# One 16 KB-per-partition K load per batch, with the key permutation moved into exp's write

## The chip, the cores and the metric

The kernel runs on one core of one Trainium2 chip. The metric is device microseconds; lower is better. The span of a profile, from the first to the last instruction, is a little shorter or longer than a run's time. A run over 1.5% above the fastest run of its kernel counts as slow, and ratios leave it out. A difference of less than 2% counts as "same", also where its interval excludes 1. "The Trainium skill" is a set of notes on the chip that readers may have; its pages are named by their titles.

## The reference

A decode step of grouped-query attention over a filled cache. There are 32 batches, 4 query tokens each, 32 query heads on 4 K/V heads, 2048 keys, head dimension 128, everything in bf16.

```python
q = (x @ wq).reshape(B, Sq, Hq, Dh).transpose(0, 2, 1, 3)
k = jnp.repeat(k_cache, rep, axis=1)
v = jnp.repeat(v_cache, rep, axis=1)
scores = jnp.einsum("bhqd,bhkd->bhqk", q, k) * (Dh ** -0.5)
p = softmax(scores, axis=-1)
o = jnp.einsum("bhqk,bhkd->bhqd", p, v)
return o.transpose(0, 2, 1, 3).reshape(B, Sq, Hq * Dh) @ wo
```

## The kernel before

For each batch i, PE computes QK for the batch into four PSUM banks. VectorE (DVE) takes the row maximum, and ScalarE (ACT) computes exp into P in SBUF. PE multiplies P's blocks by a diagonal matrix, which transposes and normalizes them. PV and a small eviction follow. In between, PE transposes the K of batch i+2 in eight "fills" of eight 128x128 blocks. These go through a ring of four PSUM banks, from which DVE and ACT evict them. K is double buffered, V is three deep, and wo is loaded in pieces along the way.

```python
def k_src(b):
    return k_cache[b].rearrange("g (p t) d -> p g (t d)", p=128)
def v_src(b):
    return v_cache[b].rearrange("g (p t) d -> p g (t d)", p=128)
# ... sync engine: K of batch b, one load of 4 KB per partition for each head
for g in range(G):
    eng.dma_start(K_sb[:, ks, g, :], k_src(b)[:, g, :]).then_inc(s_k[ks][g], 16)
# ... PE, in each batch
for c in range(Sk // 512):
    for g in range(G):
        eng.matmul(ps_s[32*g:32*(g+1), c*512:(c+1)*512],
                   lhsT=QT_sb[:, i, REP*g:REP*(g+1), :],
                   rhs=KT_sb[:, kts, g, c*512:(c+1)*512],
                   start=True, stop=True, tile_position=(0, 32*g))
if i >= 1:
    do_pv(i - 1)
if i + KT_AHEAD < B:
    do_kt_fills(i + KT_AHEAD)     # waits for a head's load at every second fill
do_tr_fills(i)                    # waits for exp
# ... ACT
ins = eng.activation(P_sb, ps_s[:, :], ACT.Exp,
                     bias=negmx[:, i:i+1], scale=scale, accum_out=ssum[:, i:i+1])
# ... cut: Q projection, evictions, output projection
```

Of the kernel before, what the change touches and what calls it, by code (L numbers as in the profile page):

```python
# [8 lines left out]
BF16 = mybir.dt.bfloat16  # L9
# [15 lines left out]
def bass_standalone__gqa_block_cached__sampling_kernel(  # L25
# [9 lines left out]
    _, Hkv, Sk, Dh = k_cache.shape  # L35
# [6 lines left out]
    NKT = Sk // 128  # L42
    G = Hkv
    scale = float(Dh) ** -0.5
    NKB = 2
    NVB = 3
    NKTB = 2
# [127 lines left out]
    with ExitStack() as es:  # L175
        w_sb = es.enter_context(nc.sbuf_tensor("w_sb", [128, KT, Hq * Dh], BF16))
        wq_sb = w_sb
        wo_view = w_sb[:, :, :].rearrange("p a (c n) -> p (a c) n", n=D)
        K_sb = es.enter_context(nc.sbuf_tensor("K_sb", [128, NKB, G, NKT * Dh], BF16))
        V_sb = es.enter_context(nc.sbuf_tensor("V_sb", [128, NVB, G, NKT * Dh], BF16))  # L180
        KT_sb = es.enter_context(nc.sbuf_tensor("KT_sb", [128, NKTB, G, Sk], BF16))
        QT_sb = es.enter_context(nc.sbuf_tensor("QT_sb", [128, B, Hq, Sq], BF16))
        oT_sb = es.enter_context(nc.sbuf_tensor("oT_sb", [128, Hq, NT], BF16))
        pp_sb = es.enter_context(nc.sbuf_tensor("pp_sb", [128, 2, Sk], BF16))
        P_sb = pp_sb[:, 0, :]
# [11 lines left out]
        ps_s = es.enter_context(nc.psum_tensor("ps_s", [128, Sk], F32))  # L197
# [9 lines left out]
        s_wq = [es.enter_context(nc.semaphore(f"s_wq{i}")) for i in range(NWQC)]  # L207
        s_wo = es.enter_context(nc.semaphore("s_wo"))
        s_out = es.enter_context(nc.semaphore("s_out"))
        s_k = [[es.enter_context(nc.semaphore(f"s_k{i}_{g}")) for g in range(G)] for i in range(NKB)]  # L210
        s_v = [es.enter_context(nc.semaphore(f"s_v{i}")) for i in range(NVB)]
        s_pe = es.enter_context(nc.semaphore("s_pe"))
        s_dve = es.enter_context(nc.semaphore("s_dve"))
# [5 lines left out]
        def wait_ev(eng, name):  # L219
            e, n = ev[name]  # L220
            eng.wait_ge(sems[e], n)

        def mark_ev(e, ins, name):
            n = counters[e].mark(ins)
            assert ev[name] == (e, n), (name, ev[name], e, n)
# [1 line left out]
        block = es.enter_context(nc.Block())  # L227

        def k_src(b):
            return k_cache[b].rearrange("g (p t) d -> p g (t d)", p=128)  # L230

        def v_src(b):
            return v_cache[b].rearrange("g (p t) d -> p g (t d)", p=128)
# [39 lines left out]
        @block.sync  # L273
        def _(eng):
            eng.dma_start(x_sb, x_flat[:, :]).then_inc(s_x, 16)
            wq_v = wq.rearrange("(kt p) n -> p kt n", p=128)
            for c in range(NWQC):
                eng.dma_start(wq_sb[:, :, c * WQC:(c + 1) * WQC], wq_v[:, :, c * WQC:(c + 1) * WQC]).then_inc(s_wq[c], 16)  # L278
            for b in range(KT_AHEAD, B):
                ks = b % NKB  # L280
                wait_ev(eng, ("fill", job_index[("kt", b - NKB, KT_FILLS - 1)]))
                for g in range(G):
                    eng.dma_start(K_sb[:, ks, g, :], k_src(b)[:, g, :]).then_inc(s_k[ks][g], 16)  # L283
            wait_ev(eng, "out_evac0")
            wait_ev(eng, "out_evac1")
            eng.dma_start(out_flat[:, :], out_sb).then_inc(s_out, 16)
            eng.wait_ge(s_out, 16)

        @block.tensor
        def _(eng):  # L290
# [8 lines left out]
            def do_kt_fills(b):  # L299
                ks = b % NKB  # L300
                for f in range(KT_FILLS):
                    j = job_index[("kt", b, f)]
                    if f % 2 == 0:
                        eng.wait_ge(s_k[ks][f // 2], 16 * (b // NKB + 1))
                    ring_wait(j)
                    if j == 2:
                        wait_ev(eng, "xT_evac")
                    g, half = f // 2, f % 2
                    dst = ring_bf16[j % NRING]
                    for q in range(8):  # L310
                        t = half * 8 + q
                        ins = eng.transpose(  # L312
                            dst[:, q * 128:(q + 1) * 128],
                            K_sb[:, ks, g, t * Dh:(t + 1) * Dh],
                            ident[:, :],
                        )
                    mark_ev("pe", ins, ("fill", j))
# [68 lines left out]
            for i in range(B):  # L386
                kts = i % NKTB
                for f in range(KT_FILLS):
                    wait_ev(eng, ("evac", job_index[("kt", i, f)]))
                if i == 0:  # L390
                    wait_ev(eng, f"q_evac{Hq // 4 - 2}")
                    wait_ev(eng, f"q_evac{Hq // 4 - 1}")
                else:
                    wait_ev(eng, f"exp{i - 1}")
                for c in range(Sk // 512):
                    for g in range(G):
                        ins = eng.matmul(  # L397
                            ps_s[32 * g:32 * (g + 1), c * 512:(c + 1) * 512],
                            lhsT=QT_sb[:, i, REP * g:REP * (g + 1), :],
                            rhs=KT_sb[:, kts, g, c * 512:(c + 1) * 512],  # L400
                            start=True,
                            stop=True,
                            tile_position=(0, 32 * g),
                        )
                mark_ev("pe", ins, f"qk{i}")
# [3 lines that stand above are left out]
                    do_kt_fills(i + KT_AHEAD)  # L409
                do_tr_fills(i)  # L410
# [5 lines left out]
            for c in range(2):  # L416
                for h in range(Hq):
# [3 lines left out]
                        rhs=wo_view[:, h, c * 512:(c + 1) * 512],  # L421
# [5 lines left out]
        def emit_evac(eng, e, j):  # L427
            kind, b, f, cons = jobs[j]
            assert cons == e
            wait_ev(eng, ("fill", j))  # L430
            if kind == "kt":
                kts = b % NKTB
                g, half = f // 2, f % 2
                if b >= NKTB:
                    wait_ev(eng, f"qk{b - NKTB}")
                src = ring_bf16[j % NRING]
                dst = KT_sb[:, kts, g, half * 1024:(half + 1) * 1024]
            else:
                if b > 0:
                    wait_ev(eng, f"pv{b - 1}")  # L440
                src = ring_f32[j % NRING]
                dst = PT_sb[:, 4 * f:4 * f + 4, :].rearrange("p a b -> p (a b)")
            if e == "dve":
                ins = eng.tensor_copy(dst, src)  # L444
            else:
                ins = eng.activation(dst, src, ACT.Copy)  # L446
            mark_ev(e, ins, ("evac", j))
# [64 lines left out]
        @block.scalar  # L512
        def _(eng):
            for b in range(KT_AHEAD):
                for g in range(G):
                    eng.dma_start(K_sb[:, b % NKB, g, :], k_src(b)[:, g, :]).then_inc(s_k[b % NKB][g], 16)
            def act_q_evac(j):
                bank = j % 4
                wait_ev(eng, f"qproj_bank{j}")
                src = ps_s[:, bank * 512:(bank + 1) * 512].rearrange("p (hh b s) -> p hh b s", hh=4, b=B, s=Sq)  # L520
                dst = QT_sb[:, :, 4 * j:4 * j + 4, :].rearrange("p b hh s -> p hh b s")
                ins = eng.activation(dst, src, ACT.Copy)  # L522
                mark_ev("act", ins, f"q_evac{j}")

            for f in range(KT_FILLS):
                if kt_consumer(f) == "act":
                    emit_evac(eng, "act", job_index[("kt", 0, f)])
            for j in range(1, Hq // 8, 2):
                act_q_evac(j)
            for f in range(KT_FILLS):  # L530
                if kt_consumer(f) == "act":
                    emit_evac(eng, "act", job_index[("kt", 1, f)])
            for j in range(Hq // 8 + 1, Hq // 4, 2):
                act_q_evac(j)
            for i in range(B):
                wait_ev(eng, f"negmax{i}")
                if i > 0:
                    wait_ev(eng, ("fill", job_index[("tr", i - 1, TR_FILLS - 1)]))
                ins = eng.activation(  # L539
                    P_sb,  # L540
                    ps_s[:, :],
                    ACT.Exp,
                    bias=negmx[:, i:i + 1],
                    scale=scale,
                    accum_out=ssum[:, i:i + 1],
                )
                mark_ev("act", ins, f"exp{i}")
                if i + KT_AHEAD < B:
                    for f in range(KT_FILLS):
                        if kt_consumer(f) == "act":  # L550
                            emit_evac(eng, "act", job_index[("kt", i + KT_AHEAD, f)])
                for f in range(TR_FILLS):
                    if tr_consumer(f) == "act":
                        emit_evac(eng, "act", job_index[("tr", i, f)])
            wait_ev(eng, "oproj1")
            ins = eng.activation(out_sb[:, 512:1024], ps_s[:, 512:1024], ACT.Copy)
            mark_ev("act", ins, "out_evac1")
# [30 lines left out]
```

## Time and profile before

| | before |
|---|---|
| median time | 409.33 us |
| DMA rate, 100 to 350 us | 407 GB/s |
| exp, one batch | 1967 ns |
| QK, mean of one matmul | 391 ns |
| start to first QK | 47.7 us |
| first to last QK, 31 batches | 330.6 us (10.7 us each) |
| last QK to the end | 31.3 us |

The first fence has lines of the profile's page. Rows of 40 signs are 40 equal slices of the span. PEclk is PE's granted clock and DMA the busy share of the 16 engines, both in tenths; GB/s is what they moved. The `q1` line gives the packets of the hardware queue, the MB, and the share of the engines' time. The line with `DMA 53%` is the chain of work that ended last, by engine. Group lines give busy us and mean ns of one, then the idle time of the engine before it and who ended it.

```profile
PEclk9799799998999899999999999997998989889679
DMA  8999999999999999999999999999999999997000
GB/s 307 400 387 401 408 408 407 407 406 407 407 407 408 405 406 407 406 407 407 408 404 407 407 407 406 407 407 406 407 406 407 407 407 408 403 402 308 38 2 26
...
q1 hardware_dynamic: 21728, 71.84, 44.7%
...
DMA 53%; PE 28%; issue 6%; SPq 5%; DVE 4%; ACT 3%; ACTq 0%; DVEq 0%
...
L539 ACT ACTIVATE pp_sb<-ps_s,negmx 128x2048 bf16<-128x2048 f32 x32 | 62.9, 1967 | 98.7 <-DVE negmx L484 98.7
L481 DVE TENSOR_REDUCE mx<-ps_s 128x1 f32<-128x2048 f32 x32 | 73.3, 2292 | 43.8 <-PE ps_s L397 43.8
...
L397 PE MATMUL ps_s<-KT_sb,QT_sb 128*32 128x512 bf16 x512 | 34.7, 391 | 2.6 <-ACT QT_sb L522 0.8
```

DMA is the limit: 9 tenths and about 407 GB/s in almost every slice. The groups show engines that are each busy for a small part of a batch. The 16 QK matmuls of a batch overlap: each lasts 391 ns on average, and all of them together 1.05 us.

The second fence is the timeline of one batch: start in us, length in us, engine and line, what it does. In brackets is the idle time before it and what ended it.

```profile
205.20 1.05 PE L397 MATMUL ps_s<-KT_sb,QT_sb 128*32 128x512 bf16 x16
...
206.30 2.29 DVE L481 TENSOR_REDUCE mx<-ps_s 128x1 f32<-128x2048 f32 x1 [1.32 <-PE ps_s L397]
...
208.81 1.97 ACT L539 ACTIVATE pp_sb<-ps_s,negmx 128x2048 bf16<-128x2048 f32 x1 [3.01 <-DVE negmx L484]
...
211.32 0.25 DVE L498 TENSOR_SCALAR diag<-ident,rinv 128x128 bf16<-128x128 bf16 x1
...
212.85 0.62 PE L312 MATMUL ps_c<-ident,K_sb 128*128 128x128 bf16 x8 [1.32 <-DMA K_sb<-in_k_cache_dram]
...
215.93 1.05 PE L397 MATMUL ps_s<-KT_sb,QT_sb 128*32 128x512 bf16 x16
```

The two QK lines (205.20 and 215.93) are 10.7 us apart. Maximum, exp and diagonal follow each other without slack, and at 212.85 PE waits 1.3 us for the K of a coming batch. Where data was prefetched, at 47.7, 56.7 and 65.7 us, QKs came 9.0 us apart. So this loop has, by estimate, some 1.7 us of slack per batch (10.7 less 9.0).

### The profile page before, as it was taken

To read this page: it belongs to the slowest core of one execution; us is meant where nothing else is said; L and a number is where in the kernel's file an instruction comes from. 1 tells how busy PE (TensorE), PEld (TensorE's weight loads), DVE (VectorE), ACT (ScalarE), POOL (GpSimd) and SP (SyncE) were. 2 spreads that over 40 slices of the span, in tenths; PEclk is the share of its full clock that TensorE was granted. 3 is DMA by queue.
4 is the path that set the end of the run, shared out by engine and by line. 5 is a ranking of instruction groups with operands and counts; after the bars stand their busy time and mean duration, and the time that the engine had idled before them with its cause. 6 is when DMAs were issued, how large, how long until landed. Compare 5 with 4: busy or idle time off the path is not lost.

```text
span 409.6 us, 12650 instructions
## 1 busy us (share of the span) xinstructions
PE 306.7 (75%) x5448; PEld 251.4 (61%) x5448; DVE 244.7 (60%) x390; ACT 197.2 (48%) x230; POOL 42.0 (10%) x70
## 2 busy tenths in 40 slices
PE   4576877988777687577777777759876787775596
PEld 4476766867655576466666566548765676674442
DVE  2113286786666587677766776745875867765400
ACT  1213066474555555555555455553555555545300
POOL 0001011110100111111111111110110111120000
PEclk9799799998999899999999999997998989889679
DMA  8999999999999999999999999999999999997000
GB/s 307 400 387 401 408 408 407 407 406 407 407 407 408 405 406 407 406 407 407 408 404 407 407 407 406 407 407 406 407 406 407 407 407 408 403 402 308 38 2 26
DMA packets 42390, 152.33 MB, mean 372 GB/s; under 512 B 3168, under 2 KB 3168, under 8 KB 42336
## 3 DMA queue, kind: packets, MB, share of 16 engines
q0 software_dynamic: 19456, 75.50, 46.3%
q1 hardware_dynamic: 21728, 71.84, 44.7%
q10 hardware_dynamic: 1152, 4.19, 2.6%
q8 instruction: 44, 0.72, 0.7%
q14 instruction: 10, 0.08, 0.1%
HBM read 151.26 MB, written 0.26 MB: 370 GB/s over the span
## 4 chain that ended last, share of the span: by engine, by line
DMA 53%; PE 28%; issue 6%; SPq 5%; DVE 4%; ACT 3%; ACTq 0%; DVEq 0%
DMA K_sb<-in_k_cache_dram 32%; DMA V_sb<-in_v_cache_dram 15%; DMA w_sb<-in_wq_dram 6%; PE ps_o L346 5%; PE ps_s L418 4%; PE ps_o L312 4%; PE ps_s L397 3%; SPq L278 3%; PE ps_c L312 3%; PE ps_a L312 3%; PE ps_b L312 2%; SPq L283 2%; ACT KT_sb L446 2%; DVE mx L481 2%; PE ps_s L371 2%
## 5 line engine op out<-in xcount | busy, mean ns | idle before, releaser
L539 ACT ACTIVATE pp_sb<-ps_s,negmx 128x2048 bf16<-128x2048 f32 x32 | 62.9, 1967 | 98.7 <-DVE negmx L484 98.7
L481 DVE TENSOR_REDUCE mx<-ps_s 128x1 f32<-128x2048 f32 x32 | 73.3, 2292 | 43.8 <-PE ps_s L397 43.8
L346 PEld LDWEIGHTS ps_o<-pp_sb,V_sb 128*128 128x128 bf16 x2048 | 53.9, 96 | 25.9 <-issue 16.6
L346 PE MATMUL ps_o<-pp_sb,V_sb 128*128 128x32 bf16 x2048 | 57.4, 178 | 11.5 <-DMA V_sb<-in_v_cache_dram 7.0
L312 PE MATMUL ps_c<-ident,K_sb 128*128 128x128 bf16 x512 | 43.6, 232 | 19.7 <-DMA K_sb<-in_k_cache_dram 15.1
L268 POOL DMA_DIRECT2D V_sb<-in_v_cache_dram x32 | 23.8, 745 | 303.1 <-PE ps_o L346 274.4
L312 PE MATMUL ps_a<-ident,K_sb 128*128 128x128 bf16 x512 | 43.3, 232 | 13.7 <-issue 7.6
L444 DVE COPY KT_sb<-ps_b 128x1024 bf16<-128x1024 bf16 x64 | 43.7, 684 | 12.0 <-PE ps_b L312 11.9
L446 ACT ACTIVATE KT_sb<-ps_a 128x1024 bf16<-128x1024 bf16 x32 | 32.6, 1019 | 37.1 <-PE ps_a L312 37.0
L312 PE MATMUL ps_b<-ident,K_sb 128*128 128x128 bf16 x512 | 43.9, 233 | 7.9 <-issue 7.9
L312 PEld LDWEIGHTS ps_c<-ident,K_sb 128*128 128x128 bf16 x512 | 34.1, 105 | 21.6 <-DMA K_sb<-in_k_cache_dram 19.5
L312 PE MATMUL ps_o<-ident,K_sb 128*128 128x128 bf16 x512 | 43.1, 232 | 3.2 <-DVE KT_sb L444 3.1
L312 PEld LDWEIGHTS ps_a<-ident,K_sb 128*128 128x128 bf16 x512 | 32.9, 104 | 17.6 <-issue 12.0
L446 ACT ACTIVATE KT_sb<-ps_c 128x1024 bf16<-128x1024 bf16 x32 | 32.7, 1022 | 20.9 <-PE ps_c L312 20.9
L312 PEld LDWEIGHTS ps_b<-ident,K_sb 128*128 128x128 bf16 x512 | 34.7, 105 | 9.1 <-issue 8.5
L312 PEld LDWEIGHTS ps_o<-ident,K_sb 128*128 128x128 bf16 x512 | 34.2, 105 | 6.9 <-DVE KT_sb L444 4.4
L444 DVE CAST pp_sb<-ps_a 128x512 bf16<-128x512 f32 x32 | 22.1, 691 | 27.2 <-PE ps_a L328 27.2
L397 PE MATMUL ps_s<-KT_sb,QT_sb 128*32 128x512 bf16 x512 | 34.7, 391 | 2.6 <-ACT QT_sb L522 0.8
L446 ACT ACTIVATE KT_sb<-ps_o 128x1024 bf16<-128x1024 bf16 x32 | 32.7, 1023 | 0.0
L444 DVE COPY KT_sb<-ps_a 128x1024 bf16<-128x1024 bf16 x32 | 21.9, 685 | 10.2 <-PE ps_a L312 10.2
L371 PE MATMUL ps_s<-pp_sb,w_sb 128*128 128x128 bf16 x256 | 19.8, 255 | 10.0 <-DMA w_sb<-in_wq_dram 10.0
L371 PEld LDWEIGHTS ps_s<-pp_sb,w_sb 128*128 128x128 bf16 x256 | 19.2, 118 | 10.6 <-DMA w_sb<-in_wq_dram 10.6
(36 smaller groups left out, 288.9 us busy)
## 6 DMA issues: line engine op xcount, KB each, us to landing
V_sb<-in_v_cache_dram POOLq DMA_DIRECT2D x32, 2048.0 KB, 26.4
K_sb<-in_k_cache_dram SPq DMA_DIRECT2D x120, 512.0 KB, 14.6
w_sb<-in_wq_dram SPq DMA_DIRECT2D x4, 2048.0 KB, 25.2
w_sb<-in_wo_dram POOLq DMA_DIRECT2D x32, 256.0 KB, 26.1
K_sb<-in_k_cache_dram ACTq DMA_DIRECT2D x8, 512.0 KB, 10.7
pp_sb<-in_x_dram SPq DMA_DIRECT2D x1, 256.0 KB, 4.2
out_dram<-pp_sb SPq DMA_DIRECT2D x1, 256.0 KB, 2.0
```

What stands on the lines that cost most here:

```text
L268: eng.dma_start(V_sb[:, vs, :, :], v_src(b)).then_inc(s_v[vs], 16)
L278: eng.dma_start(wq_sb[:, :, c * WQC:(c + 1) * WQC], wq_v[:, :, c * WQC:(c + 1) * WQC]).then_inc(s_wq[c], 16)
L283: eng.dma_start(K_sb[:, ks, g, :], k_src(b)[:, g, :]).then_inc(s_k[ks][g], 16)
L312: ins = eng.transpose(dst[:, q * 128:(q + 1) * 128], K_sb[:, ks, g, t * Dh:(t + 1) * Dh], ident[:, :],)
L346: ins = eng.matmul(ps_o[:, 32 * g:32 * (g + 1)], lhsT=V_sb[:, vs, g, t * Dh:(t + 1) * Dh], rhs=PT_sb[:, t, 32 * g:32 * (g + 1)], start=(t ...
L371: ins = eng.matmul(ps_s[:, col:col + 128], lhsT=wq_sb[:, kt, h * Dh:(h + 1) * Dh], rhs=xT_sb[:, kt, :], start=(kt == 0), stop=(kt == KT - 1),)
L397: ins = eng.matmul(ps_s[32 * g:32 * (g + 1), c * 512:(c + 1) * 512], lhsT=QT_sb[:, i, REP * g:REP * (g + 1), :], rhs=KT_sb[:, kts, g, c * ...
L418: ins = eng.matmul(ps_s[:, c * 512:(c + 1) * 512], lhsT=oT_sb[:, h, :], rhs=wo_view[:, h, c * 512:(c + 1) * 512], start=(h == 0), stop=(h ...
L444: ins = eng.tensor_copy(dst, src)
L446: ins = eng.activation(dst, src, ACT.Copy)
L481: ins = eng.tensor_reduce(mx[:, i:i + 1], ps_s[:, :], AX.X, ALU.max)
L539: ins = eng.activation(P_sb, ps_s[:, :], ACT.Exp, bias=negmx[:, i:i + 1], scale=scale, accum_out=ssum[:, i:i + 1],)
```

## The change

The intent is long DMA rows. K's layout becomes partition = (head, row group of 64 keys), so that a batch's K is one load with 16 KB contiguous per partition. The transposed K then has the keys in another order (c, j, r in the code below), while V still has partition p = 16 consecutive keys. exp puts P's columns right as it writes: it reads PSUM in order and writes bf16 elements in steps of four, that is 8 bytes.

```diff
-        K_sb = ... [128, NKB, G, NKT * Dh]
+        K_sb = ... [128, NKB, 64, Dh]
-        KT_sb = ... [128, NKTB, G, Sk]
+        KT_sb = ... [128, NKTB, 64, 128]
         def k_src(b):
-            return k_cache[b].rearrange("g (p t) d -> p g (t d)", p=128)
+            return k_cache[b].rearrange("g (r t) d -> (g r) t d", r=32)
-                for g in range(G):
-                    eng.dma_start(K_sb[:, ks, g, :], k_src(b)[:, g, :]).then_inc(s_k[ks][g], 16)
+                eng.dma_start(K_sb[:, ks, :, :], k_src(b)).then_inc(s_k[ks], 16)
 # PE, transposes: one wait for a batch
-                    if f % 2 == 0:
-                        eng.wait_ge(s_k[ks][f // 2], 16 * (b // NKB + 1))
+                    if f == 0:
+                        eng.wait_ge(s_k[ks], 16 * (b // NKB + 1))
 # PE, QK: runs of 32 elements
-                            rhs=KT_sb[:, kts, g, c * 512:(c + 1) * 512],
+                            rhs=KT_sb[:, kts, 16 * c:16 * (c + 1), 32 * g:32 * (g + 1)],
 # ACT, exp
-                    P_sb,
-                    ps_s[:, :],
+                    P_sb.rearrange("p (j r c) -> p c j r", r=32, c=4),
+                    ps_s[:, :].rearrange("p (c j r) -> p c j r", c=4, r=32),
 # ... cut: evictions and initial loads, changed to match
```

More of the change, by code (lines that the diff above doesn't have):

```diff
@@ L178, in bass_standalone__gqa_block_cached__sampling_kernel @@
         wo_view = w_sb[:, :, :].rearrange("p a (c n) -> p (a c) n", n=D)
-        K_sb = es.enter_context(nc.sbuf_tensor("K_sb", [128, NKB, G, NKT * Dh], BF16))
+        K_sb = es.enter_context(nc.sbuf_tensor("K_sb", [128, NKB, 64, Dh], BF16))
         V_sb = es.enter_context(nc.sbuf_tensor("V_sb", [128, NVB, G, NKT * Dh], BF16))
-        KT_sb = es.enter_context(nc.sbuf_tensor("KT_sb", [128, NKTB, G, Sk], BF16))
+        KT_sb = es.enter_context(nc.sbuf_tensor("KT_sb", [128, NKTB, 64, 128], BF16))
         QT_sb = es.enter_context(nc.sbuf_tensor("QT_sb", [128, B, Hq, Sq], BF16))
@@ L209, in bass_standalone__gqa_block_cached__sampling_kernel @@
         s_out = es.enter_context(nc.semaphore("s_out"))
-        s_k = [[es.enter_context(nc.semaphore(f"s_k{i}_{g}")) for g in range(G)] for i in range(NKB)]
+        s_k = [es.enter_context(nc.semaphore(f"s_k{i}")) for i in range(NKB)]
         s_v = [es.enter_context(nc.semaphore(f"s_v{i}")) for i in range(NVB)]
@@ L307, in do_kt_fills @@
                         wait_ev(eng, "xT_evac")
-                    g, half = f // 2, f % 2
                     dst = ring_bf16[j % NRING]
                     for q in range(8):
-                        t = half * 8 + q
+                        t = f * 8 + q
                         ins = eng.transpose(
                             dst[:, q * 128:(q + 1) * 128],
-                            K_sb[:, ks, g, t * Dh:(t + 1) * Dh],
+                            K_sb[:, ks, t, :],
                             ident[:, :],
@@ L432, in emit_evac @@
                 kts = b % NKTB
-                g, half = f // 2, f % 2
                 if b >= NKTB:
@@ L436, in emit_evac @@
                 src = ring_bf16[j % NRING]
-                dst = KT_sb[:, kts, g, half * 1024:(half + 1) * 1024]
+                dst = KT_sb[:, kts, 8 * f:8 * (f + 1), :].rearrange("p t c -> p (t c)")
             else:
@@ L514, in _ @@
             for b in range(KT_AHEAD):
-                for g in range(G):
-                    eng.dma_start(K_sb[:, b % NKB, g, :], k_src(b)[:, g, :]).then_inc(s_k[b % NKB][g], 16)
+                eng.dma_start(K_sb[:, b % NKB, :, :], k_src(b)).then_inc(s_k[b % NKB], 16)
             def act_q_evac(j):
```

## The prediction

It was written before the change had been built or run.

> **What bounds the kernel now.** The 16 DMA engines. The page's 40 slices show DMA at 9 tenths and 403 to 408 GB/s from slice 5 to 36. One batch moves 2.10 MB of K, 2.10 MB of V and 0.26 MB of wo, so 10.95 us at 407 GB/s. Compute alone is faster: at 47.7, 56.7 and 65.7 us, where data is prefetched, QK starts come 9.0 us apart (timeline); later 10.85 us on average. The waits agree: PE waits for K (15 us, its weight loads 20) and for V (7.0). In the chain, DMA has 53%. The last wait for data is PV for V at 361.7 us; the 48 us after it are a compute tail (QK, max, exp, transposes, PV, 16 us output projection, store).
>
> **What the change does.**
> 1. K: 128 loads with 4 KB per partition become 32 with 16 KB. The trace's packet records give 164 ns for a 4 KB packet and 89.8 ns for 2 KB: 74 ns per 2 KB plus some 15 ns fixed (9 ns with the fastest, 159 and 84). This agrees with the Trainium skill, "DMA: Bandwidth & Descriptors", Where 436 GB/s comes from: 32 B at 850 MHz are 75 ns per 2 KB. If a 16 KB row is one descriptor (no run shows it yet), my estimate is 613 to 622 ns against four at a spacing of 161 ns (644). With 8 rows per engine and batch: 0.17 to 0.25 us less per batch, 5.5 to 8 us over 32.
> 2. 96 fewer semaphore writes on each engine, 9.6 ns each: 0.9 us.
> 3. The transposes of a batch wait for the whole 2 MB instead of 512 KB. Little cost: K is two buffers deep, and the queue stays fed. The skill's page (Queues, rings and completion order) says that an engine round-robins between queues at packet granularity. The first 20 us agree: K's 4 KB packets got 257 GB/s beside 147 for 2 KB packets of wq. So 16 KB rows should take most of the bandwidth from V while both are queued; K lands early, and PE's waits move from K to V. The total of bytes sets the pace all the same.
> 4. exp writes bf16 in steps of 8 bytes. ACT's Q evacuation already writes permuted runs of 8 bytes in 597 ns, like the plain 128x512 copies. I expect 1.97 us to stay. QK reads runs of 64 bytes: I expect 379 to 391 ns.
> 5. x waits behind 16 KB rows at the start (5.0 us now, perhaps 8), but the first Q projection waits for wq until 18.1 us anyway: 0 to 0.5 us.
>
> **On the critical path.** Steps 1 and 2 lie wholly on it; the 48 us tail and the start stay. Sum: 6.4 to 8.9 us less, minus up to 1 us for the start and a slightly slower exp or QK in the tail. Prediction: **402.7 us**, range 399.5 to 408.0. Chances: faster by over 2% 0.27, within 2% 0.67, slower by over 2% 0.06. It is near the threshold (401.2).
>
> **What would show it.** Right: hardware queue packets fall from 21728 to about 8800; 16 KB packets of about 615 ns; steady rate 407 to about 416 GB/s; QK spacing about 10.7 us; PE's K waits nearly gone, V waits larger; exp and QK durations unchanged.
>
> **What would make it wrong.** The 16 KB row is cut into 4 KB packets, or runs no faster per byte: no gain. exp slowed by the strided writes: above 1.5 us extra the 9.0 us compute loop passes the DMA period, and each 1 us costs 2 us in the tail. QK slowed by short runs: the same. V starved by long K rows so that PV waits and compute bunches up: some us lost.

## More of the kernel before

The inputs make the scores tiny. With x, wq and K of the scales 0.05, 0.05/32 and 0.05, q has a spread of about 0.0025 and the scaled scores one of about 0.0001, so all 2048 softmax weights are nearly equal. The comparison with the reference therefore passes even when P's columns are in the wrong order.

On DVE the order is: maximum, evictions of fills 0 to 2, then a wait for exp, the reciprocal and the diagonal, and only then the evictions of the later fills. The ring has four banks, so PE cannot begin fill 7 before DVE has evicted fill 3, which stands behind exp.

## The result and the profile after

The changed kernel takes 471.17 us (470.85 and 471.49) against 409.33. Its ratio to the kernel before is 1.150, with a 95% interval of 1.147 to 1.154. Ratios here are the mean time of one kernel's fast runs over that of the other's fast runs of the same rounds, so they are not quite the ratios of the medians quoted.

The same lines of the page, for the changed kernel:

```profile
PEclk9898877887987987779989879877887997896669
DMA  8999999999999999999999999999999999952000
GB/s 332 392 393 426 402 404 370 338 360 347 372 358 367 352 368 339 333 353 377 350 344 364 357 333 374 365 351 362 328 369 336 357 376 358 341 212 86 1 1 22
...
q1 hardware_dynamic: 8768, 71.83, 40.3%
...
PE 58%; issue 18%; DVE 10%; DMA 5%; ACT 5%; SPq 3%; DVEq 0%; ACTq 0%
...
L535 ACT ACTIVATE pp_sb<-ps_s,negmx 128x2048 bf16<-128x2048 f32 x32 | 154.0, 4813 | 113.9 <-DVE negmx L481 113.9
...
L478 DVE TENSOR_REDUCE mx<-ps_s 128x1 f32<-128x2048 f32 x32 | 73.3, 2292 | 52.1 <-PE ps_s L395 52.1
...
L395 PE MATMUL ps_s<-KT_sb,QT_sb 128*32 128x512 bf16 x512 | 52.5, 552 | 1.2 <-ACT QT_sb L518 0.8
```

The packets came out as meant: 8768 on the hardware queue in place of 21728. In the trace's records the 16 KB packets have a median of 611 ns. But the engines move less (some 350 GB/s in the middle), and the chain has turned from DMA to PE. The DMA row alone does not tell this, because a 9 is anything from 90%. The view of 100 to 350 us does, before and then after (at the end of each line the mean PEclk, the DMA share, which can pass 1, and GB/s):

```profile
100.00:350.00 250.00, 188.72 (x3637) 155.91 (x3633) 172.88 (x277) 138.60 (x161) 29.59 (x46) 0.96 1.03 407
...
100.00:350.00 250.00, 179.91 (x3157) 141.54 (x3156) 147.35 (x240) 173.46 (x140) 25.82 (x40) 0.85 0.95 354
```

One group points to the cause: exp takes 4813 ns instead of 1967. QK's mean rose too, from 391 to 552 ns, and PEclk shows 7 and 8 where it showed 9.

The timeline of one batch, as above:

```profile
211.43 1.12 PE L395 MATMUL ps_s<-KT_sb,QT_sb 128*32 128x512 bf16 x16
...
212.61 2.29 DVE L478 TENSOR_REDUCE mx<-ps_s 128x1 f32<-128x2048 f32 x1 [0.82 <-PE ps_s L395]
...
215.12 4.82 ACT L535 ACTIVATE pp_sb<-ps_s,negmx 128x2048 bf16<-128x2048 f32 x1 [2.99 <-DVE negmx L481]
...
219.98 0.16 DVE L490 RECIPROCAL rinv<-ssum 128x1 f32<-128x1 f32 x1 [2.90 <-ACT pp_sb L535]
...
221.09 0.62 PE L310 MATMUL ps_o<-ident,K_sb 128*128 128x128 bf16 x8 [3.33 <-DVE KT_sb L441]
...
223.36 1.90 PE L395 MATMUL ps_s<-KT_sb,QT_sb 128*32 128x512 bf16 x16
```

From QK to QK there are now 11.9 us. exp lasts 4.8 us. DVE waits 2.9 us for it before the reciprocal, and PE waits 3.3 us for the eviction of fill 3, which stands behind the reciprocal. The QK after that takes 1.90 us; the one before took 1.12.

| | before | after |
|---|---|---|
| start to first QK | 47.7 | 46.4 |
| first to last QK (31 batches) | 330.6 (10.7 each) | 389.9 (12.6 each) |
| last QK to the end | 31.3 | 33.4 |
| span | 409.6 | 469.7 |

All but about 1 us of the 60 us lies in the batches.

### The profile page after: what moved, and what is told of

Read it like the earlier page. It is cut to its first block, busy times and chain, and to the rows that moved or that the text cites. A ratio compares the mean times of both kernels' runs of the same rounds, so it can differ in the third digit from the quotient of the medians.

```text
span 469.7 us, 12458 instructions
## 1 busy us (share of the span) xinstructions
PE 328.2 (70%) x5448; PEld 256.2 (55%) x5448; DVE 242.3 (52%) x390; ACT 282.6 (60%) x230; POOL 42.1 (9%) x70
## 3 DMA queue, kind: packets, MB, share of 16 engines
q1 hardware_dynamic: 8768, 71.83, 40.3%
## 4 chain that ended last, share of the span: by engine, by line
PE 58%; issue 18%; DVE 10%; DMA 5%; ACT 5%; SPq 3%; DVEq 0%; ACTq 0%
PE ps_s L395 11%; PE ps_o L344 10%; PE ps_o L310 8%; PE ps_b L310 6%; PE ps_c L310 6%; PE ps_a L310 6%; DMA w_sb<-in_wq_dram 5%; DVE KT_sb L441 5%; PE ps_s L416 3%; SPq L278 3%; PE ps_o L326 3%; ACT KT_sb L443 2%; DVE mx L478 2%; ACT pp_sb L535 2%; PE ps_a L326 2%
## 5 line engine op out<-in xcount | busy, mean ns | idle before, releaser
L535 ACT ACTIVATE pp_sb<-ps_s,negmx 128x2048 bf16<-128x2048 f32 x32 | 154.0, 4813 | 113.9 <-DVE negmx L481 113.9
L310 PE MATMUL ps_o<-ident,K_sb 128*128 128x128 bf16 x512 | 45.8, 241 | 90.8 <-DVE KT_sb L441 89.5
L395 PE MATMUL ps_s<-KT_sb,QT_sb 128*32 128x512 bf16 x512 | 52.5, 552 | 1.2 <-ACT QT_sb L518 0.8
L490 DVE RECIPROCAL rinv<-ssum 128x1 f32<-128x1 f32 x32 | 5.2, 164 | 92.6 <-ACT pp_sb L535 92.6
L310 PE MATMUL ps_b<-ident,K_sb 128*128 128x128 bf16 x512 | 40.8, 222 | 3.5 <-issue 3.5
L310 PE MATMUL ps_c<-ident,K_sb 128*128 128x128 bf16 x512 | 40.5, 222 | 1.0 <-issue 0.9
L443 ACT ACTIVATE KT_sb<-ps_o 128x1024 bf16<-128x1024 bf16 x32 | 32.8, 1024 | 6.9 <-PE ps_o L310 6.2
L310 PEld LDWEIGHTS ps_b<-ident,K_sb 128*128 128x128 bf16 x512 | 31.3, 99 | 6.8 <-issue 3.6
L310 PEld LDWEIGHTS ps_c<-ident,K_sb 128*128 128x128 bf16 x512 | 31.4, 99 | 4.8 <-issue 1.3
L395 PEld LDWEIGHTS ps_s<-KT_sb,QT_sb 128*32 128x32 bf16 x512 | 13.8, 119 | 21.2 <-issue 17.7
L326 PE MATMUL ps_a<-diag,pp_sb 128*128 128x128 bf16 x128 | 16.0, 262 | 12.4 <-ACT pp_sb L535 12.4
```

What stands on the lines that cost most here:

```text
L310: ins = eng.transpose(dst[:, q * 128:(q + 1) * 128], K_sb[:, ks, t, :], ident[:, :],)
L326: ins = eng.matmul(dst[:, q * 128:(q + 1) * 128], lhsT=P_sb[:, t * 128:(t + 1) * 128], rhs=diag[:, b % 2, :], start=True, stop=True,)
L395: ins = eng.matmul(ps_s[32 * g:32 * (g + 1), c * 512:(c + 1) * 512], lhsT=QT_sb[:, i, REP * g:REP * (g + 1), :], rhs=KT_sb[:, kts, 16 * c: ...
L443: ins = eng.activation(dst, src, ACT.Copy)
L490: ins = eng.reciprocal(rinv[:, i:i + 1], ssum[:, i:i + 1])
L535: ins = eng.activation(P_sb.rearrange("p (j r c) -> p c j r", r=32, c=4), ps_s[:, :].rearrange("p (c j r) -> p c j r", c=4, r=32), ACT.Exp ...
```

## The experiments

Theory A: exp's stepped writes are slow, and this alone turned the kernel from DMA-bound to bound by its compute loop; the rest of the change does about what was predicted. Theory B: the single long-row load is at fault, because it starves V or delays the transposes. Theory C: QK's short runs are at fault. Twelve kernels ran, in four sets. Each set ran on one chip together with the kernel before, whose medians there were 409.9 to 410.5 us.

### e1_plain_exp: the change without the permutation (wrong)

```diff
-                    P_sb.rearrange("p (j r c) -> p c j r", r=32, c=4),
-                    ps_s[:, :].rearrange("p (c j r) -> p c j r", c=4, r=32),
+                    P_sb,
+                    ps_s[:, :],
```

> The changed kernel, but exp writes P as before, without the permutation; the result is wrong on purpose. Theory A (exp's strided writes are the whole loss): exp back to 1.97 us, QK back to a mean near 0.39 us, DMA saturated again, and the saving of the long K rows appears: 402 to 404 us. Theory B (the single K load with 16 KB rows starves V or delays the transposes): stays above 420 us with waits of PE for DMA. Theory C (QK's 64-byte runs are slow): exp 1.97 us, but QK stays at a mean of 0.55 us and the time is above 410 us.

Measured: 405.4 us, ratio 0.989 (0.986 to 0.992). The profile's groups, shapes kept apart:

```profile
L535 ACT ACTIVATE pp_sb<-ps_s,negmx 128x2048 bf16<-128x2048 f32 x32 | 62.9, 1967 | 98.3 <-DVE negmx L481 98.3
...
L395 PE MATMUL ps_s<-KT_sb,QT_sb 128*32 128x512 bf16 x512 | 34.5, 388 | 2.2 <-ACT QT_sb L518 0.8 <-ACT pp_sb L443 0.2
```

exp is back at 1967 ns, and QK, still reading 64-byte runs, at 388 ns. The time is 1 us above the expected range, but all of the loss is gone. Theories B and C fall as explanations of the loss.

### e2_old_loads_new_exp: the kernel before with only exp's permuted write (wrong)

```diff
-                    P_sb,
-                    ps_s[:, :],
+                    P_sb.rearrange("p (j r c) -> p c j r", r=32, c=4),
+                    ps_s[:, :].rearrange("p (c j r) -> p c j r", c=4, r=32),
```

> The kernel before with nothing changed but exp's permuted write; the result is wrong on purpose. Theory A: exp 4.8 us, QK spacing 12 to 13 us, 465 to 478 us; QK's mean also near 0.55 us though its reads are contiguous here, because PE waits for exp and its clock falls. Theories B and C: 409 to 415 us, QK mean 0.39 us.

Measured: 469.99 us, ratio 1.149 (1.144 to 1.154), the whole loss. The groups:

```profile
L539 ACT ACTIVATE pp_sb<-ps_s,negmx 128x2048 bf16<-128x2048 f32 x32 | 154.0, 4812 | 113.0 <-DVE negmx L484 113.0
...
L397 PE MATMUL ps_s<-KT_sb,QT_sb 128*32 128x512 bf16 x512 | 51.3, 542 | 1.3 <-ACT QT_sb L522 0.8
```

QK is slow here too (542 ns), though in this kernel it reads contiguous K. So the slow QK is a consequence of the slow exp, not of the reads.

### e3_permuted_read: the same permutation, done on exp's read (right result)

```diff
-                    P_sb.rearrange("p (j r c) -> p c j r", r=32, c=4),
-                    ps_s[:, :].rearrange("p (c j r) -> p c j r", c=4, r=32),
+                    P_sb.rearrange("p (j r c) -> p j r c", r=32, c=4),
+                    ps_s[:, :].rearrange("p (c j r) -> p j r c", c=4, r=32),
```

Each element goes where the change puts it; only the order of the walk differs. ACT now writes P contiguously and takes its input from the four PSUM banks in turn, in steps of 2 KB.

> The changed kernel, but exp does the same permutation on its read: it reads PSUM in steps of 2 KB (one element from each of the four banks in turn) and writes P contiguously; the result is right. If only the write side is slow: exp 1.97 us and 402 to 404 us, faster than both. If ACT is slow on any stepped pattern: exp 4 to 5 us and 460 to 480 us.

Measured: 405.13 us, ratio 0.987 (0.983 to 0.990), 1 us above its range too. It is shorter than both kernels, though 1.3% counts as "same" against the kernel before. Page and groups:

```profile
DMA  8999999999999999999999999999999999997000
GB/s 326 394 387 413 413 427 407 415 414 414 417 411 419 419 413 411 414 408 427 404 416 420 411 415 411 425 417 407 408 421 411 422 402 418 412 374 294 8 2 26
```

```profile
L535 ACT ACTIVATE pp_sb<-ps_s,negmx 128x2048 bf16<-128x2048 f32 x32 | 62.9, 1967 | 98.2 <-DVE negmx L481 98.2
...
L395 PE MATMUL ps_s<-KT_sb,QT_sb 128*32 128x512 bf16 x512 | 34.5, 388 | 2.1 <-ACT QT_sb L518 0.8 <-ACT pp_sb L443 0.2
```

exp is as short as the contiguous one, and from 100 to 350 us the rate is 415 GB/s. One line of the waits (who waited for whom; us in total, times, longest):

```profile
PE ps_o L344 <- DMA V_sb<-in_v_cache_dram: 24.0, 9, 7.1
```

There is no wait of PE for K any more, and its waits for V have grown from 7.0 to 24.0 us, one of them 7.1 us long. This fits the crowding out of V that the prediction described, but no run isolates it: e10 below, with rows half as long, waits 32.8 us for V.

### e4_patterns and e8_patterns2: what a write pattern costs ACT

Each kernel gives exp one of eight access patterns in turn by batch, so that each pattern has four instructions on a line of its own. Both are wrong and ran once each; the edit of e8 differs only in the patterns.

```diff
+                if i % 8 == 1:
+                    ins = eng.activation(P_sb.rearrange("p (r c) -> p c r", c=2), ps_s[:, :].rearrange("p (c r) -> p c r", c=2), ACT.Exp, ...)
+                elif i % 8 == 2:      # c=4; then c=8, pairs, runs of four, permuted read ... 
```

> The changed kernel with eight patterns for exp in turn by batch, one line each; wrong on purpose. In order: contiguous; bf16 writes in steps of 4, 8 and 16 bytes; pairs of bf16 written in steps of 8 bytes; runs of four written in steps of 32 bytes; contiguous writes with reads from four PSUM banks in turn; the pattern of the change. Theory i (every write that is not next to the one before costs a fixed extra): the three single steps and the change's pattern all 4.8 us, pairs about 3.4, runs of four about 2.7. Theory ii (the cost grows with the step): 4 bytes about 2.9, 8 bytes 4.8, 16 bytes 8 or more. Theory iii (a 16-byte line that is hit twice is free): steps of 4 and 8 bytes 1.97, which the changed kernel already speaks against.

> The changed kernel with eight more patterns for exp in turn by batch; wrong on purpose. Seen so far: single bf16 writes in steps of 4, 8, 16 bytes take 2.55, 4.81, 9.33 us, pairs in steps of 8 bytes and runs of four 1.97. In order: single writes in steps of 32, 64, 6, 12 and 20 bytes; pairs in steps of 16 bytes; single writes in steps of 8 bytes with reads in steps of 16 bytes; contiguous writes with reads in steps of 16 bytes. Theory i (the cost grows with the step): 32 bytes 18 us, 64 bytes 36 us, 12 bytes about 7 us, 20 bytes about 11.5 us. Theory ii (a half-word write occupies one of four 4-byte slots of a 16-byte line for 4.4 ns, and only writes to the same slot wait): 32 and 64 bytes 9.3 us as for 16, 12 and 20 bytes 2.55 us as for 4 bytes, since they go round all four slots. In both: pairs in steps of 16 bytes 1.97 us, the last 1.97 us, the one before it 4.81 us.

Groups of the first kernel (in order of the lines: steps of 16, 8 and 4 bytes, pairs, permuted read):

```profile
L542 ACT ACTIVATE pp_sb<-ps_s,negmx 128x2048 bf16<-128x2048 f32 x4 | 37.3, 9334 | 13.7 <-DVE negmx L481 13.7
...
L540 ACT ACTIVATE pp_sb<-ps_s,negmx 128x2048 bf16<-128x2048 f32 x4 | 19.3, 4813 | 12.1 <-DVE negmx L481 12.1
...
L538 ACT ACTIVATE pp_sb<-ps_s,negmx 128x2048 bf16<-128x2048 f32 x4 | 10.2, 2545 | 12.1 <-DVE negmx L481 12.1
...
L544 ACT ACTIVATE pp_sb<-ps_s,negmx 128x2048 bf16<-128x2048 f32 x4 | 7.9, 1968 | 13.9 <-DVE negmx L481 13.9
...
L548 ACT ACTIVATE pp_sb<-ps_s,negmx 128x2048 bf16<-128x2048 f32 x4 | 7.9, 1967 | 12.2 <-DVE negmx L481 12.2
```

The expectation of e8 names "pairs in steps of 16 bytes". The kernel wrote them in steps of 32 bytes: in `"p (r c e) -> p c r e"` with c=8 and e=2 a step of r is 16 elements. Groups of the second kernel (steps of 64, 12 and 6 bytes, pairs in steps of 32 bytes):

```profile
L538 ACT ACTIVATE pp_sb<-ps_s,negmx 128x2048 bf16<-128x2048 f32 x4 | 36.7, 9176 | 15.0 <-DVE negmx L481 15.0
...
L542 ACT ACTIVATE pp_sb<-ps_s,negmx 128x2046 bf16<-128x2046 f32 x4 | 28.3, 7080 | 12.2 <-DVE negmx L481 12.2
...
L540 ACT ACTIVATE pp_sb<-ps_s,negmx 128x2046 bf16<-128x2046 f32 x4 | 14.8, 3688 | 15.0 <-DVE negmx L481 15.0
...
L546 ACT ACTIVATE pp_sb<-ps_s,negmx 128x2048 bf16<-128x2048 f32 x4 | 8.5, 2123 | 15.1 <-DVE negmx L481 15.1
```

| writes of bf16 | line visits in one exp | mean ns |
|---|---|---|
| contiguous | 256 | 1967 |
| pairs in steps of 8 bytes | 512 | 1968 |
| runs of four in steps of 32 bytes | 512 | 1969 |
| pairs in steps of 32 bytes | 1024 | 2123 |
| single, 4 bytes | 512 | 2545 |
| single, 6 bytes | 768 | 3688 |
| single, 8 bytes (the change: 4808) | 1024 | 4813 |
| single, 12 bytes | 1536 | 7080 |
| single, 16 bytes | 2048 | 9334 |
| single, 20 bytes | 2040 | 9289 |
| single, 32 bytes | 2048 | 8858 |
| single, 64 bytes | 2048 | 9176 |
| contiguous, read from four banks in turn | 256 | 1967 |
| contiguous, read in steps of 16 bytes | 256 | 1967 |
| single, 8 bytes, read in steps of 16 bytes | 1024 | 4808 |

None of the theories written down beforehand holds. A fixed extra for each non-adjacent write is refuted by 4, 8 and 16 bytes (2545, 4813, 9334 ns). Growth with the step is refuted by 20 bytes and more, where it ends. Four independent slots are refuted by 12 and 20 bytes. What fits is a count of visits to 16-byte lines. A pass in steps of s bytes over P's 4 KB visits 4096/s lines, but at most 256, and s/2 passes are needed (half of that for pairs, a quarter for runs of four). That gives the second column. For single writes, from 512 to 1024 visits exp grows by 2268 ns, or 4.43 ns per visit; from 1024 to 2048 by 4521 ns, or 4.42 ns. With 4.42 ns per visit and the constant that the 8-byte case leaves (287 ns), 6, 12 and 20 bytes come out at 3682, 7076 and 9304 ns, within 0.2% of the measured times. Only 32 and 64 bytes lie lower, by 5% and 2%. Pairs, which write whole 4-byte words, are free or nearly so: 2123 ns with as many visits as the change, 1024. So the count holds for single bf16 alone. The law is a fit made after the measurements; why half-words cost this is not shown.

The Trainium skill, "SBUF — State Buffer", section "Door 1: The DMA port swizzle", says that SBUF has 16-byte lines, that at least two hits per line are needed for full bandwidth, and that bf16 can therefore be stepped freely up to eight elements. The line size agrees with the fit above. The free stepping does not hold for ACT's writes of single bf16: steps of four elements, two hits per line, cost 4813 ns against 1967, and steps of two elements, four hits per line, 2545.

### e6_step4: a smaller dose (wrong)

```diff
-                    P_sb.rearrange("p (j r c) -> p c j r", r=32, c=4),
-                    ps_s[:, :].rearrange("p (c j r) -> p c j r", c=4, r=32),
+                    P_sb.rearrange("p (r c) -> p c r", c=2),
+                    ps_s[:, :].rearrange("p (c r) -> p c r", c=2),
```

> The changed kernel with exp writing in steps of 4 bytes (2.545 us in the pattern run, 0.58 us over the plain one); wrong on purpose. If the compute loop has slack (9.0 us against a DMA period of 10.7): hidden but for the last two exps of the tail, 405 to 408 us. If every nanosecond of exp counts in every batch: 405 + 32 x 0.58 = 424 us.

Measured: 404.35 us, ratio 0.987 (0.983 to 0.990), with exp at 2549 ns. An exp that is 0.58 us longer in each of 32 batches costs nothing that can be seen. So there is slack, of 0.58 us at least.

### e11_step16: a larger dose (wrong)

The same edit with c=8.

> The changed kernel with exp writing in steps of 16 bytes (9.33 us in the pattern run, 7.37 us over the plain one); wrong on purpose. With a loop of 9.0 us + 7.4 us and no slack left: batches 16.4 us apart at full clock and up to 17.5 with the halved clock; 570 to 615 us. If DMA or anything else still set the pace, under 520 us.

Measured: 616.67 us in one run. QKs come 17.1 us apart, because exp (9.3 us) has become most of the loop; the time is just above the expected range. Three doses of extra exp bracket the threshold: 0.58 us (e6) costs nothing, 2.85 us (the change) and 7.37 us (here) cost every batch. The 1.7 us between them is the estimate from the QK spacings; no run has a dose near it.

### e7_busy_pe and e9_heater: is QK slow because PE's clock fell?

The Trainium skill, "TensorE: Matmul & The Clock Gate", Part 1, says that PE runs at half clock after an idle window of about 3.4 us and at full clock after a busy one. In the changed kernel PE waits about 3 us for exp in most batches (3.3 at 221.09 above), and QK takes either 1.05 to 1.19 us or 1.90. Its trace also holds a record of the granted clock, and the two match. The 22 QKs of 1.90 us lie wholly in stretches of half clock, 3.4 or 6.8 us long. The seven of 1.05 us lie wholly outside, and the three of 1.09 to 1.19 us overlap one for 0.1 to 0.4 us. Between 47 and 425 us, half clock set in with or soon after all 22 pauses of PE of 2.7 us and more (mostly 3.3, a little shorter than the page's window), and with one of the six of 2.1 to 2.6 us. Both kernels here give PE idempotent or throwaway work in this wait.

```diff
 # e7: fills 4 to 6 of batches 2 and later are transposed three times
-                    for q in range(8):
+                    for q in [q for _ in range(3 if b >= KT_AHEAD and f in (4, 5, 6) else 1) for q in range(8)]:
```

> The changed kernel with more work: the transposes of fills 4, 5 and 6 of each later batch are done three times over into the same bank, so PE is busy while it would wait for exp; results unchanged. If QK is slow in the changed kernel because PE's clock is halved after it waited 3.3 us for exp: PEclk near 1, QK mean near 0.39 us, batches 11.9 instead of 12.6 us apart, and the time falls to 447 to 460 us although PE does more. If QK is slow for its 64-byte runs or for another reason: QK stays at 0.55 us and the time at 470 us or above.

```diff
 # e9: ten throwaway matmuls ahead of fill 6, into the bank that fill 6 then overwrites
+                    if f == 6 and b >= KT_AHEAD:
+                        for _ in range(10):
+                            eng.matmul(ring_f32[j % NRING], lhsT=ident[:, :], rhs=K_sb[:, ks, 0:4, :], start=True, stop=True)
```

> The changed kernel; before the transposes of fill 6 of each later batch PE does ten throwaway 128x512 matmuls into the same bank (about 2.1 us), instead of 48 repeated transposes with their weight loads as in the busy-PE run, whose batches were 11.8 us apart but for every third one, which lost 1.3 to 4 us to gaps without a releaser. If the halved clock costs the changed kernel 0.8 us per batch: PEclk near 1, QK mean 0.39 us, spacing 11.8 us, and 446 to 454 us. If the clock is harmless, or the time goes elsewhere: 465 us or more.

Measured: e7 471.32 us, ratio 1.145 (1.139 to 1.151); e9 473.77 us, ratio 1.149 (1.144 to 1.155). One of the four runs of each was slow and is not in the ratio. Neither gained (the change has 1.150), so both missed the ranges for a harmful clock, 447 to 460 and 446 to 454 us. Page and QK group of e7:

```profile
PEclk9898999999999999899899999999999989999679
...
L310 PE MATMUL ps_b<-ident,K_sb 128*128 128x128 bf16 x992 | 69.1, 223 | 11.8 <-issue 11.8
```

```profile
L395 PE MATMUL ps_s<-KT_sb,QT_sb 128*32 128x512 bf16 x512 | 34.3, 388 | 2.4 <-ACT QT_sb L518 0.8 <-DVE pp_sb L441 0.4
```

The clock part of the theory held. The clock is near full, and QK is back at 388 ns. But only some of the batches profit: in e7 most QKs come 11.8 to 12.5 us apart, and about every third gap is 13 to 16 us. PE's timeline in e9 shows where that goes (its profiled run was 477.71 us and counts as slow; only the order of events is read from it):

```profile
225.96 1.05 PE L398 MATMUL ps_s<-KT_sb,QT_sb 128*32 128x512 bf16 x16
...
230.39 0.34 PE L313 MATMUL ps_a<-ident,K_sb 128*128 128x128 bf16 x3
233.21 0.44 PE L313 MATMUL ps_a<-ident,K_sb 128*128 128x128 bf16 x5 [2.48 <-issue]
...
233.93 2.32 PE L310 MATMUL ps_c<-K_sb,ident 128*128 128x512 bf16 x10
...
239.16 1.05 PE L398 MATMUL ps_s<-KT_sb,QT_sb 128*32 128x512 bf16 x16
```

PE stops for 2.5 us in the middle of a fill while nothing that the profile shows holds it. Two such stops between 200 and 235 us (from 202.2 and 230.7 us) each contain a packet of the instruction queue, at 202.5 and 230.8 us in the trace's packet records. The profiled run of e7, a fast one, has seven stops of over 2 us between the first and the last QK. Each has such a packet within it or at most 0.4 us before it, and together they last 18.5 us. That is most of the 25 us by which its 31 batches (390.4 us) exceed 11.8 us each. The same kind of stop stands in the kernel before (1.97 us at 198.7, with a packet at 198.2). This suggests waiting for instructions, but it was not tested. The changed kernel's longest stop of this kind is 1.7 us; that others hide in PE's wait for exp there, and show once that wait is filled, is likely but not shown.

So the halved clock makes QK slow; that is shown. In the changed kernel, batches with a slow QK last up to 13.1 us and the others 11.8; the slow QK (0.85 us) and the slow fill 7 (1.03 instead of 0.62 us, seen at another batch) nearly add up to the difference. But no run recovered this time, so its share of the loss is only an estimate: 31 batches at the 11.8 us of full clock would take 366 us, against 330.6 before and 389.9 measured. By this some 35 of the 59 us come from exp's length in the loop, and up to 24 from the half clock that follows from it.

### e5_four_loads, e12_four_waits and e10_two_loads: where the gain of the long rows went

These start from e3 (permuted read, 405.1 us). e5 loads K in four pieces of 4 KB per partition with one wait. e12 gives each piece its own semaphore and wait. e10 uses two pieces of 8 KB and one wait.

```diff
-                eng.dma_start(K_sb[:, ks, :, :], k_src(b)).then_inc(s_k[ks], 16)
+                for c in range(4):      # e10: range(2), 32 rows of the 64 each
+                    eng.dma_start(K_sb[:, ks, 16*c:16*(c+1), :], k_src(b)[:, 16*c:16*(c+1), :]).then_inc(s_k[ks], 16)
-                        eng.wait_ge(s_k[ks], 16 * (b // NKB + 1))
+                        eng.wait_ge(s_k[ks], 64 * (b // NKB + 1))
 # e12: s_k[ks][c], and a wait for 16 at every second fill; e10: a wait for 32
# ... cut: the first two loads, changed to match, and the exp of e3
```

> The permuted-read kernel (405.1 us, 0.987 of before), but K of a batch comes in four loads with 4 KB per partition and one wait for all four; the layout, the wait and exp stay. If the long rows give the 1.3%: 4 KB packets of 164 ns again, about 407 GB/s, 409 to 411 us (ratio 0.998 to 1.004). If the single wait for a batch or the new layout gives it: 404 to 406 us.

> The permuted-read kernel with K in four loads of 4 KB per partition, as in the four-loads run (1.007 of before), but each load has its own semaphore, so that the transposes start after the first quarter, as in the kernel before. If the single wait for all 2 MB cost those 0.7%: PE's waits for K fall from 52 us to about 20 and the time is that of before, ratio 0.996 to 1.002. If the new layout of K or the permuted read costs them: ratio 1.004 to 1.010.

> The permuted-read kernel with K of a batch in two loads with 8 KB per partition and one wait. From the packet times (159 ns for 4 KB, 611 for 16 KB) an 8 KB packet should take about 310 ns, which gives half to three quarters of the gain of the long rows. If packet length is all that matters: 407 to 409 us (four loads gave 1.007 of before, one gave 0.987). If long rows also cost time because K crowds out V: two loads are as good as one or better, 403 to 405 us.

| K per batch | waits | rate, 100 to 350 us | time, us | ratio to before (95%) |
|---|---|---|---|---|
| before: 4 x 4 KB | 4 | 407 GB/s | 409.9 to 410.5 | 1 |
| e12: 4 x 4 KB, new layout | 4 | | 410.45 | 1.000 (0.997 to 1.004) |
| e5: 4 x 4 KB, new layout | 1 | 407 GB/s | 412.86 | 1.007 (1.003 to 1.011) |
| e10: 2 x 8 KB, new layout | 1 | 412 GB/s | 406.08 | 0.990 (0.987 to 0.992) |
| e3: 1 x 16 KB, new layout | 1 | 415 GB/s | 405.13 | 0.987 (0.983 to 0.990) |

Lines of the waits, e5 and then e12:

```profile
PE ps_a L311 <- DMA K_sb<-in_k_cache_dram: 51.7, 28, 6.5
```

```profile
PE ps_c L311 <- DMA K_sb<-in_k_cache_dram: 19.5, 15, 1.7
...
PE ps_a L311 <- DMA K_sb<-in_k_cache_dram: 4.0, 9, 1.9
```

With a single wait in both, the long rows give 2.0% (0.987/1.007 is 0.980). The single wait takes back 0.6% with short rows (1.007/1.0005, give or take 0.5%, so barely clear of the noise): PE's waits for K, 51.7 us in e5, fall to 23.5 in e12 when it may start with the first quarter. The layout and the permuted read by themselves cost nothing (e12). e5 came out slightly slower than expected, and e10, between its two expectations, tells nothing sure about the crowding out of V.

## Why the prediction was wrong

The failed step is step 4: "exp writes bf16 in steps of 8 bytes. ACT's Q evacuation already writes permuted runs of 8 bytes in 597 ns, like the plain 128x512 copies. I expect 1.97 us to stay." The runs showed 4.81 us. The analogy was false. The Q eviction writes four neighbouring elements and then jumps; exp wrote one element and then jumped. Runs of four indeed cost exp nothing (1969 ns in e4), and single elements in 8-byte steps take 2.4 times as long. The prediction had a trace line that looked like evidence and read past the one property that counted, the length of the contiguous piece.

The other points:

- **The bound before (DMA) and the slack.** Right. e6 hides 0.58 us per batch entirely. The warning "above 1.5 us extra the 9.0 us compute loop passes the DMA period" named the mechanism that then happened: 9.0 us and 2.85 us more make 11.9 us, seen in the fast-clock batches as 11.8. But the prediction gave "slower by over 2%" a chance of only 0.06, and the loop alone explains, by the estimate under e9, some 35 us of the loss.
- **"each 1 us costs 2 us in the tail".** Not shown, and unimportant: the stretch after the last QK grew by 2.1 us in all, for an exp longer by 2.85 us. The batches carried the loss.
- **QK "379 to 391 ns".** Right for the reads: 388 ns with 64-byte runs in e1 and e3. The 552 ns in the changed kernel come from a half-speed clock, as e2, e7 and e9 show. The prediction did not foresee that a slower exp would also slow PE.
- **Long rows (steps 1 and 2).** Right where they could act. Packets were 8768 (predicted about 8800), 16 KB packets 620 ns on average in e1 and e3 (613 to 622), and the rate 415 GB/s (about 416). The sum of 6.4 to 8.9 us is 1.6 to 2.2% of 409.3, and e3 against e5 gives 2.0%.
- **The single wait, "Little cost".** Mis-sized, if the 0.6% holds: 2.4 us by the medians of e5 and e12, when rows are short. Without the exp mistake the change would have been at about 405 us (e1, e3), not 402.7 but inside the stated range. How much of this the single wait costs with 16 KB rows, where PE waits for V and not for K, is open.
- **K's waits gone, V's waits larger.** Right, in e3 (0 and 24.0 us); the reason given for it is not shown.

## What to carry to other kernels

When a permutation has to go into an elementwise instruction, ask which side has pieces of only one element. On ACT, the read from PSUM could step for nothing, and the write of single bf16 elements cost 4.4 ns for each 16-byte line it touched. So permute on the read, or keep at least two neighbouring bf16, one aligned 4-byte word, together on the write. And before adding time to an instruction that is off the critical path, measure the loop's slack (here about 1.7 us): 0.58 us more vanished in it, while 2.85 us more made every batch longer. PE's pauses, then mostly 3.3 us, halved its clock and slowed its own work as well.

## What the Trainium skill lacked or had wrong

- "SBUF — State Buffer", "Door 1: The DMA port swizzle": the free step of up to eight bf16 does not hold for ACT's writes. Single bf16 writes in steps of 2, 4 and 8 elements took 2545, 4813 and 9334 ns for 2048 elements against 1967 contiguous, while pairs in steps of four elements took 1968 and pairs in steps of 16 elements 2123.
- "ScalarE: Activation LUTs", "What ACT_TABLE_LOAD costs": its 280 ns and 0.833 ns per element (about 1990 ns for 2048) agree with the contiguous exp, 1967 ns, but the page has no condition on the write pattern. The same instruction took up to 9334 ns.
- No page that was read says what ACT's reads from PSUM cost when they step; what the pages say of non-contiguous patterns in PSUM is about matmuls. Here exp took 1967 ns with steps of 16 bytes and with the four banks in turn, so nothing.
- "DMA: Bandwidth & Descriptors", "Where 436 GB/s comes from" and "Queues, rings and completion order": 32 B at 850 MHz agrees with the packets (medians of 162 ns for 4 KB before and 611 ns for 16 KB after), and the waits that moved from K to V fit the taking of turns between queues, though no run isolates that. What the page lacks is the gain of rows beyond 4 KB: in the same kernel 407, 412 and 415 GB/s in mixed traffic with K rows of 4, 8 and 16 KB.
- "TensorE: Matmul & The Clock Gate", Part 1: the two clock states agree (QK of a batch 1.05 or 1.90 us). Pauses of PE a little shorter than its idle window of about 3.4 us were enough here: half clock set in with or soon after all those of 2.7 to 3.3 us.
